# Two alpha loads move behind other transfers of SyncE's queue, their logarithms move later, and chunk 2's second row is prepared ahead of its first

## The chip, the core and the metric

The kernel runs on one NeuronCore of a Trainium2 chip. The core has five instruction streams that run side by side and meet only at semaphores: TensorE (PE, matrix products; its weight loads are listed apart as PEld), VectorE (DVE), ScalarE (ACT), GpSimd (POOL) and SyncE (SP), which here only issues transfers. Transfers are carried by 16 DMA engines. POOL's transfers stand in the profile as queue q0, SP's as q1. SBUF is the on-chip memory with 128 partitions; PSUM is the accumulator memory, here one tile of 8 banks of 512 float32 per partition.

The metric is the device time of one execution in microseconds (us). Lower is better.

## The reference

Two layers follow each other. The first is a gated linear attention, a recurrence over 768 time steps for 4 batches times 8 heads with a head dimension of 48:

```python
for t in range(S):
    state = alpha[:, :, t, :, None] * state + np.einsum('bhd,bhe->bhde', k[:, :, t], v[:, :, t])
    y[:, :, t] = np.einsum('bhd,bhde->bhe', q[:, :, t], state)
```

The second takes y as 3072 tokens of width 384 through a bilinear feed-forward layer of width 1536:

```python
a = x @ w_a
b = x @ w_b
return (a * b @ w_out)
```

q, k, v and alpha are 4 x 8 x 768 x 48 float32 (alpha between 0.8 and 1.0), w_a and w_b are 384 x 1536, w_out is 1536 x 384, and the output is 3072 x 384 float32.

## The kernel before

**Tiling.** The work is cut into six chunks, numbered 0 to 5. A chunk holds 256 time steps of two batches; the two batches are its "rows" 0 and 1 (the argument `u`, and `*` for both). Chunks 0 and 1 hold the first 256 steps of batches 0, 1 and of 2, 3; chunks 2 and 3 the next 256 steps; chunks 4 and 5 the last. A chunk thus needs the state that the chunk two before it left.

**One chunk, stage by stage.** The recurrence is turned into matrix products. The alphas of a chunk are loaded (`ld a`, line 413, one transfer of 768 KB for both rows) and their logarithms taken on ACT (`ln`, line 420). Pairs of neighbouring steps are added on DVE (`lx`, lines 433 and 436: three additions), split into a part that is exact in bf16 and two rests (`R 0` and `R 1`, line 497, on DVE: `lh` and `ll`), and summed along time by TensorE (`AQ`, line 507). Exponentials of the sums on ACT give the factors `beta` and `invb` (`E`, line 541). Queries and keys of even steps are first levelled with one alpha (`lv`, line 526, on POOL or DVE; `ra`, line 519, is the reciprocal that the queries take) and then multiplied by `beta` and `invb` on DVE (`mq` and `mk`, line 552), which gives the bf16 tile `QKp`. One transposing transfer per row, issued by SP (`T`, line 604), turns `QKp` into `kqT`. TensorE multiplies turned keys with turned queries (`D`, line 674); ACT or DVE take the result out of PSUM (`Mc`, line 683; `M`, line 679) and DVE applies the causal mask (`Mm`, line 687). TensorE also updates the state (`KA` or `K`, line 627; `k`, lines 662 and 663, on DVE) and forms y from the carried state (`SA`, `SB`, line 703) and from the masked scores (`Y`, line 724). ACT or DVE copy y out of PSUM as bf16 (`X`, lines 764 and 766), and a second kind of transposing transfer on SP (`XT`, line 771) turns it into `xT`, the input of the feed-forward layer.

The feed-forward layer of a chunk is 12 pieces of the hidden width. For each, `a` and `b` (line 786) fill one PSUM bank each, ACT copies the first (`as`, line 792), DVE multiplies it with the second (`pr`, line 800), and `o` (line 808) makes the output, which ACT or DVE copy (`ot`, lines 823 and 825) and SP stores (`st`, line 841).

**Order.** Nothing is scheduled by a planner. The order is written out by hand in the string `PROGRAM` at the top of the file: each line starts with a chunk number, then lists operations with their row, bank or engine (V is DVE, S is ACT, P is POOL, Y is SP). The program is recorded in that order, so every engine has its instructions in the order in which `PROGRAM` names them, and each engine works strictly in its order: an instruction that waits holds everything behind it on that engine. The framework adds the waits that the data and the buffers need. The feed-forward work of one chunk is mixed with the recurrence of the next, so that TensorE always has something to do.

**Names that the change touches.** The chunk's alpha tile `a_t` has two buffers: chunk 4's alphas take the place of chunk 2's, chunk 5's that of chunk 3's. The logarithms `la`, the pair sums, `lh` and `ll` have one buffer each. `gate_t` and `gate_m` (lines 858 to 864) are one-element copies on POOL into a scratch tile; they do no work, but POOL cannot pass them before the tile that they read is written:

```python
def gate_t(x, u):

    nc.gpsimd.tensor_copy(go, x.kqT[int(u)][0:1, 0, 0, 0, 0:1])
```

In `PROGRAM` the places that matter are lines 93 to 112 (end of chunk 2's preparation, beside chunk 1's feed-forward work), 135 to 163 (chunk 2's y, chunk 3's preparation, first part of chunk 2's feed-forward work), 166 to 182 (chunk 3's recurrence) and 194 to 206 (chunk 4's preparation ends, chunk 5's begins).

Of the kernel before, what the change touches and what calls it, by code (L numbers as in the profile page):

```python
# [92 lines left out]
1: a 7 0 3; b 11 0 1; pr 11 0; KA 1 64; k 1 0 V; k 1 1 V; b 10 0 5; a 10 0 7; as 10 0; a 0 0 6  # L93
2: lv 0 k V
1: pr 10 0; b 0 0 1; a 3 0 4; as 0 0; pr 0 0
2: lv 1 k P; mk 1 V
1: as 3 0; b 3 0 7; a 1 0 6; as 1 0
4: ld a * P
1: b 7 0 0; b 1 0 4; pr 1 0; as 7 0; pr 7 0; pr 3 0
2: mk 0 V  # L100
1: SB 1 0
3: ln *
1: a 6 0 2; as 6 0; b 9 0 3; a 4 0 5; a 9 0 6; as 9 0; pr 9 0
2: mq 1 V; T 1
0: o 2 0 4
1: b 4 0 6; b 6 0 7
2: lv 0 q P; mq 0 V
1: pr 6 0
2: T 0
3: ld k * Y  # L110
# [24 lines left out]
2: D 0 0 5; Mc 0 0; Mm 0 0 V; gatem 0 0; SB 0 1; SA 1; Y 1; X 1 S; XT 1  # L135
3: lv 0 k P; lv 1 k P
1: a 4 1 7
4: ln *
1: as 4 1; b 9 1 0; pr 9 1; o 0 0 5
3: AQ 3  # L140
2: SA 0; Y 0; X 0 S; XT 0
5: ld a * Y
1: o 0 1 -; ot 0 V; a 1 1 6; a 10 1 1; as 1 1; as 10 1
3: E 0 b; E 0 i
1: b 4 1 2; pr 4 1; b 8 1 5; b 1 1 1; a 8 1 6; b 10 1 0; pr 1 1; o 3 0 2; pr 10 1; as 8 1; pr 8 1; o 3 1 -; ot 3 S; st 3 Y
# [3 lines left out]
3: E 1 i  # L149
1: st 0 Y  # L150
3: dr
4: lx V; R 0
3: mk 0 V; mq 0 V; T 0
4: ld q * Y
2: a 1 * 2; b 5 * 0; as 5 *; pr 5 *
4: ra 1
2: b 7 * 4; b 10 * 1; pr 4 *; a 10 * 6; as 10 *; pr 10 *
3: mk 1 V
2: a 7 * 0; b 1 * 5; a 0 * 6; b 0 * 7; as 1 *; as 7 *; pr 1 *; pr 7 *; as 0 *; a 3 * 0; b 9 * 1; pr 0 *
3: mq 1 V  # L160
# [5 lines left out]
3: KA * 06; D 0 0 4; M 0 0; dl; k * 0 V; k * 1 V  # L166
1: o 1 0 2
2: b 11 * 7
5: ln *
2: a 11 * 5; as 11 *; pr 11 *  # L170
1: o 1 1 -; ot 1 S
2: a 6 * 5; as 6 *; a 8 * 3; as 8 *
3: SB 0 6; D 0 1 0; M 0 1; T 1
4: ld k * Y
3: D 1 0 4; Mc 1 0
2: b 6 * 2; pr 6 *; b 8 * 3; pr 8 *
4: R 1
# [16 lines left out]
3: a 11 * 5  # L194
2: ot 2 V; ot 3 V
4: mq 0 V; mk 0 V
5: lx V
3: a 9 * 3; a 0 * 2; a 8 * 6; b 11 * 7; as 9 *; as 11 *; as 0 *; pr 11 *; b 9 * 2; b 0 * 1; pr 9 *
5: lv 0 k V
3: as 8 *  # L200
# [70 lines left out]
def kernel(  # L271
# [11 lines left out]
    nc = tc.nc  # L283
# [17 lines left out]
    ld = ctx.enter_context(tc.tile_pool(name="ld", bufs=2))  # L301
# [21 lines left out]
    go = cst.tile([1, 1], F32, name="go")  # L323
    S0 = [cst.tile([C, B, D + P2 * VS], BF16, name=f"S0{i}") for i in range(2)]
    Sm = [cst.tile([C, 2, D + P2 * VS], BF16, name=f"Sm{i}") for i in range(2)]
    QKp = [cst.tile([C, 2, 2, 2, H, DP], BF16, name=f"QKp{i}") for i in range(2)]
# [9 lines left out]
    def const_fill():  # L336
        nc.vector.memset(wz, 0.0)
        nc.vector.memset(og, 0.0)  # L338
        for g in range(2):
            nc.vector.memset(og[g * HC:(g + 1) * HC, g:g + 1], 1.0)  # L340
# [517 lines left out]
    def gate_m(x, u, h):  # L858

        nc.gpsimd.tensor_copy(go, x.m[int(u), int(h)][0:1, 0, 0, 0, 0:1])  # L860

    def gate_t(x, u):

        nc.gpsimd.tensor_copy(go, x.kqT[int(u)][0:1, 0, 0, 0, 0:1])

    OPS = {
        "gatet": gate_t,
        "gatem": gate_m,
        "c1": lambda x: const_fill(),
        "c1a": lambda x: const_table(),  # L870
# [99 lines left out]
```

## Time and profile before

| What | Value |
|---|---|
| Median of 3 runs | 194.94 us (194.47 to 197.66) |
| The profiled execution, own time | 193.93 us |
| Its span, first to last instruction | 192.2 us |
| Granted TensorE clock, mean | 0.999 of full speed |
| Busy: PE / DVE / ACT / POOL | 184.1 / 136.1 / 103.1 / 50.1 us |
| Weight loads (PEld) | 111.3 us, beside PE |
| Moved by DMA | 30.96 MB, mean 161 GB/s |

The span leaves out what lies around the first and last instruction: 193.93 - 192.2 = 1.7 us. The busy times overlap, since the engines run side by side; the share that counts is that of the engine on which the end depends. In a row of the timeline the columns are: start in us from the span's start, length in us, engine, line of the kernel and operation, what it writes and reads, shapes, and how many instructions of a kind are merged into the row; in brackets stands how long the engine had been idle before and what released it. "SPq" is SP's own queue: the length of such a row is the time that SP spent on issuing, not the transfer's. A row of the list of transfers gives tile and source, issuing queue, count, size of each, and the median us from issue to landing.

### The profile page before, as it was taken

The numbers are of one execution on the slowest core, as the hardware profiler recorded it, in microseconds if no ns is written. First come the engines' busy times: TensorE is split into PE (matmuls) and PEld (weight loads), VectorE is DVE, ScalarE is ACT, GpSimd is POOL, SyncE is SP. The second block draws the span as 40 slices with busy tenths as digits, with TensorE's granted clock in tenths as the row PEclk, the third lists the DMA queues.
The fourth block names the chain that finished last, engine by engine and source line by source line (L and its number), as shares of the span: only waits on it lengthen the run. The fifth ranks groups of instructions, "written<-read, shape, count | busy, mean of one in ns | idle before, by whom it ended". The sixth has DMA issues, their size and how long they took to land.

```text
span 192.2 us, 5878 instructions
## 1 busy us (share of the span) xinstructions
PE 184.1 (96%) x2509; PEld 111.3 (58%) x2509; DVE 136.1 (71%) x230; ACT 103.1 (54%) x189; POOL 50.1 (26%) x72
## 2 busy tenths in 40 slices
PE   7979799999999998999999999999999999999993
PEld 3567576766777875644556644555544565544562
DVE  4778767999899796688979499864953961156520
ACT  4385566887585567446566135875266521164301
POOL 8999746920641404000400020050000000000000
PEclk9999999999999999999999999999999999999999
DMA  6999999999999999949993586998196005031013
GB/s 149 246 216 215 243 241 254 249 245 261 252 233 219 191 213 248 215 126 229 151 220 54 141 185 154 160 173 111 47 198 144 3 3 123 3 108 56 2 41 123
DMA packets 67162, 30.96 MB, mean 161 GB/s; under 512 B 58064, under 2 KB 65120, under 8 KB 67136
## 3 DMA queue, kind: packets, MB, share of 16 engines
q0 software_dynamic: 18640, 14.16, 41.9%
q1 hardware_dynamic: 48352, 16.34, 40.6%
q8 instruction: 19, 0.31, 0.7%
q10 hardware_dynamic: 144, 0.10, 0.2%
q14 instruction: 7, 0.06, 0.1%
HBM read 25.98 MB, written 4.74 MB: 160 GB/s over the span
## 4 chain that ended last, share of the span: by engine, by line
PE 86%; POOL 6%; DMA 4%; issue 1%; DVE 0%; ACT 0%; POOLq 0%; DVEq 0%
PE psum L786 48%; PE psum L808 24%; DMA wb_t<-in_moe_w_b_dram 4%; PE psum L674 3%; PE psum L724 2%; PE psum L627 2%; PE psum L698 2%; PE psum L703 1%; PE psum L507 1%; PE psum L819 1%; POOL v_t L413 1%; PE psum L593 1%; POOL a_t L413 1%; POOL wa_t L393 1%; POOL k_t L413 0%
## 5 line engine op out<-in xcount | busy, mean ns | idle before, releaser
L786 PE MATMUL psum<-xT,wb_t 128*128 128x512 bf16 (+1 forms) x270 | 57.0, 337 | 0.6 <-DMA wb_t<-in_moe_w_b_dram 0.5
L786 PE MATMUL psum<-xT,wa_t 128*128 128x512 bf16 (+1 forms) x270 | 56.1, 337 | 1.1 <-issue 0.7
L808 PE MATMUL psum<-wo_t,prod 128*128 128x384 bf16 x276 | 48.5, 326 | 0.0
L786 PEld LDWEIGHTS <-wb_t 128*128 128x128 bf16 x270 | 25.5, 98 | 21.1 <-DMA wb_t<-in_moe_w_b_dram 0.8
L786 PEld LDWEIGHTS <-wa_t 128*128 128x128 bf16 x270 | 25.6, 98 | 20.8 <-issue 1.0
L808 PEld LDWEIGHTS <-prod 128*128 128x128 bf16 x276 | 26.1, 98 | 16.9
L683 ACT ACTIVATE m<-psum 128x1024 bf16<-128x1024 f32 x16 | 16.3, 1023 | 6.5 <-PE psum L674 6.3
L825 DVE COPY ot<-psum 128x384 f32<-128x384 f32 (+1 forms) x13 | 6.9, 539 | 15.9 <-PE psum L808 13.4
L526 POOL TENSOR_TENSOR q_t<-q_t,ra 128x384 f32<-128x384 f32 x8 | 8.7, 1084 | 34.3 <-DMA q_t<-in_q_dram 17.3
L823 ACT ACTIVATE ot<-psum 128x384 f32<-128x384 f32 (+1 forms) x12 | 5.7, 477 | 12.9 <-PE psum L808 11.9
L420 ACT ACTIVATE la<-a_t 128x1536 f32<-128x1536 f32 (+2 forms) x9 | 9.5, 1057 | 3.4 <-DMA a_t<-in_alpha_dram 3.4
L687 DVE TENSOR_TENSOR m<-m,mask 128x1024 bf16<-128x1024 bf16 x16 | 10.8, 685 | 0.3 <-ACT m L683 0.3
L679 DVE TENSOR_TENSOR m<-psum,mask 128x1024 bf16<-128x1024 f32 x8 | 9.8, 1222 | 1.7 <-PE psum L674 1.5
L526 POOL TENSOR_TENSOR k_t<-k_t,a_t 128x384 f32<-128x384 f32 x5 | 5.3, 1064 | 19.0 <-DVE QKp L552 17.5
L552 DVE TENSOR_TENSOR QKp<-k_t,invb 128x768 bf16<-128x768 f32 x10 | 9.9, 992 | 0.2
L552 DVE TENSOR_TENSOR QKp<-q_t,beta 128x768 bf16<-128x768 f32 x10 | 9.3, 949 | 0.0
L674 PE MATMUL psum<-kqT 64*64 64x128 bf16 x384 | 8.6, 218 | 0.5 <-DVE prod L800 0.2
L413 POOL DMA_DIRECT2D v_t<-in_v_dram x8 | 8.6, 1070 | 0.5 <-issue 0.4
L674 PEld LDWEIGHTS <-kqT 64*64 64x64 bf16 x384 | 6.3, 107 | 3.2 <-issue 2.1
L764 ACT ACTIVATE ys<-psum 128x768 bf16<-128x768 f32 x7 | 5.6, 809 | 4.3 <-PE psum L703 2.3
L413 POOL DMA_DIRECT2D a_t<-in_alpha_dram x6 | 6.3, 1042 | 4.0 <-DMA wa_t<-in_moe_w_a_dram 2.2
L446 PE MATMUL psum<-wz 128*128 128x512 bf16 x17 | 5.5, 472 | 1.2 <-DVE og L338 1.2
(273 smaller groups left out, 270.9 us busy)
## 6 DMA issues: line engine op xcount, KB each, us to landing
out_dram<-ot SPq DMA_DIRECT2D x23, 192.0 KB, 2.2
a_t<-in_alpha_dram POOLq DMA_DIRECT2D x3, 768.0 KB, 14.5
k_t<-in_k_dram SPq DMA_DIRECT2D x3, 768.0 KB, 7.2
q_t<-in_q_dram POOLq DMA_DIRECT2D x2, 768.0 KB, 13.0
v_t<-in_v_dram POOLq DMA_DIRECT2D x4, 384.0 KB, 10.1
q_t<-in_q_dram SPq DMA_DIRECT2D x2, 768.0 KB, 6.6
a_t<-in_alpha_dram POOLq DMA_DIRECT2D x3, 384.0 KB, 5.6
q_t<-in_q_dram POOLq DMA_DIRECT2D x3, 384.0 KB, 13.4
```

Of the source, the lines that this page charges most:

```text
L413: eng.dma_start(out=t[:, us, hs].rearrange("p b h r d -> p (b h) (r d)"), in_=src[ch.b0 + us.start:ch.b0 + us.stop, hs, ch.s * 2 * C:(ch.s ...
L420: nc.scalar.activation(out=ch.la[:, us, hs].rearrange("p b h r d -> p (b h r d)"), in_=ch.a[:, us, hs].rearrange("p b h r d -> p (b h r d) ...
L526: eng.tensor_mul(x, x, by)
L552: eng.tensor_mul(QKp[ch.c % 2][:, u, j, :, hs, :D], src[:, u, hs].rearrange("p h r d -> p r h d"), f)
L674: nc.tensor.matmul(s2[g * HC:(g + 1) * HC, r, p, rk, :], lhsT=ch.kqT[u][rs, 1, rk, 2 * h + p, g * HC:(g + 1) * HC], rhs=queriesT(ch, u, 2 ...
L679: nc.vector.tensor_mul(m.rearrange("p r a k s -> p (r a) (k s)"), ch.s2[u, h].rearrange("p r a k s -> p (r a) (k s)"), maskn(4))
L683: nc.scalar.activation(out=m.rearrange("p r a k s -> p (r a) (k s)"), in_=ch.s2[u, h].rearrange("p r a k s -> p (r a) (k s)"), func=AF.Copy)
L687: eng.tensor_mul(x, x, maskn(4))
L786: nc.tensor.matmul(p, lhsT=(wa_t, wb_t)[w][:, kk, f * 128:(f + 1) * 128], rhs=ch.xT[:, us.start // 2:us.stop // 2, kk].rearrange("p u g s ...
L808: nc.tensor.matmul(op, lhsT=ch.prod[:, f, at:at + C], rhs=wo_t[:, f, :], start=(f == 0), stop=(f == NFF - 1))
L823: nc.scalar.activation(out=o_, in_=i_, func=AF.Copy)
L825: eng.tensor_copy(o_, i_)
```

## The change

Five things move; no arithmetic is added or removed.

- The load of chunk 4's alphas leaves POOL, where it stood behind the levelling of chunk 2's keys, and goes to SP behind the two transposing transfers of chunk 2's y. Chunk 5's alphas, which SP loaded there, go further back on SP, behind the load of chunk 4's keys and so ahead of the transposing transfers of chunk 3's y.
- The logarithms of chunk 4 (ACT) and their pair sums (DVE) move from ahead of chunk 3's multiplications into chunk 2's feed-forward work; the first rest (`R 0`, DVE) moves behind chunk 3's first scores. `R 1` and all that follows stay.
- The logarithms of chunk 5 move from chunk 3's state update to directly ahead of their pair sums, behind chunk 4's factors.
- In chunk 2, row 1's queries are multiplied and its `QKp` turned before row 0's keys are multiplied.
- A new gate on POOL waits for chunk 2's row 1 keys in `QKp` before POOL levels row 0's queries.

TensorE's instructions keep their order.

```diff
@@ PROGRAM, chunk 2's preparation @@
 1: a 7 0 3; b 11 0 1; pr 11 0; KA 1 64; k 1 0 V; k 1 1 V; b 10 0 5; a 10 0 7; as 10 0; a 0 0 6
 2: lv 0 k V
 1: pr 10 0; b 0 0 1; a 3 0 4; as 0 0; pr 0 0
-2: lv 1 k P; mk 1 V
+2: lv 1 k P; mk 1 V; gatek 1; lv 0 q P
 1: as 3 0; b 3 0 7; a 1 0 6; as 1 0
-4: ld a * P
 1: b 7 0 0; b 1 0 4; pr 1 0; as 7 0; pr 7 0; pr 3 0
-2: mk 0 V
+2: mq 1 V; T 1
 1: SB 1 0
 3: ln *
 1: a 6 0 2; as 6 0; b 9 0 3; a 4 0 5; a 9 0 6; as 9 0; pr 9 0
-2: mq 1 V; T 1
+2: mk 0 V
 0: o 2 0 4
 1: b 4 0 6; b 6 0 7
-2: lv 0 q P; mq 0 V
+2: mq 0 V
 1: pr 6 0
 2: T 0
 3: ld k * Y
@@ chunk 2's y, chunk 3's preparation @@
 3: lv 0 k P; lv 1 k P
 1: a 4 1 7
-4: ln *
 1: as 4 1; b 9 1 0; pr 9 1; o 0 0 5
 3: AQ 3
 2: SA 0; Y 0; X 0 S; XT 0
-5: ld a * Y
+4: ld a * Y
 1: o 0 1 -; ot 0 V; a 1 1 6; a 10 1 1; as 1 1; as 10 1
...
 3: dr
-4: lx V; R 0
 3: mk 0 V; mq 0 V; T 0
 4: ld q * Y
 2: a 1 * 2; b 5 * 0; as 5 *; pr 5 *
-4: ra 1
-2: b 7 * 4; b 10 * 1; pr 4 *; a 10 * 6; as 10 *; pr 10 *
+4: ln *; ra 1
+2: b 7 * 4; b 10 * 1; pr 4 *
+4: lx V
+2: a 10 * 6; as 10 *; pr 10 *
 3: mk 1 V
@@ chunk 3's recurrence @@
 2: b 11 * 7
-5: ln *
 2: a 11 * 5; as 11 *; pr 11 *
 1: o 1 1 -; ot 1 S
 2: a 6 * 5; as 6 *; a 8 * 3; as 8 *
+4: R 0
 3: SB 0 6; D 0 1 0; M 0 1; T 1
 4: ld k * Y
+5: ld a * Y
 3: D 1 0 4; Mc 1 0
@@ chunk 5's preparation @@
 4: mq 0 V; mk 0 V
-5: lx V
+5: ln *; lx V
@@ the new gate @@
+    def gate_k(x, u):
+
+        nc.gpsimd.tensor_copy(go, QKp[x.c % 2][0:1, int(u), 1, 0, 0, 0:1])
+
+        "gatek": gate_k,
```

## The prediction

> **What bounds the kernel now.** I read the page's head and the shares of the chain that ended last first, then that chain in order of time.
>
> ```profile
> span 192.2 us, 5878 instructions
> PE 184.1 (96%) x2509; PEld 111.3 (58%) x2509; DVE 136.1 (71%) x230; ACT 103.1 (54%) x189; POOL 50.1 (26%) x72
> ...
> PE 86%; POOL 6%; DMA 4%; issue 1%; DVE 0%; ACT 0%; POOLq 0%; DVEq 0%
> ```
>
> TensorE is the bound: busy 184.1 of 192.2 us. Nothing else holds over 1% of the chain except POOL and the DMA, whose parts, as the chain shows, lie before 22.6 us. So an edit to loads, logarithms or queues can only move the end through an idle gap of TensorE that it closes or opens. The chain shows where those gaps are (start, length, what):
>
> ```profile
> 22.61 0.05 issue
> ...
> 60.63 4.96 PE psum L786 x45
> ...
> 66.14 0.63 PE psum L674 x32
> ...
> 76.32 0.72 issue
> ...
> 98.65 0.46 PE psum L674 x32
> ...
> 104.42 0.51 PE psum L724 x32
> ...
> 110.88 9.06 PE psum L786 x42
> ```
>
> From 22.6 us on the chain is TensorE's own work, with two gaps: one from 60.63 + 4.96 = 65.59 to 66.14, and one of 0.72 at 76.32 in which TensorE waits for nothing that the profile shows. The first lies inside the region of the change. Together they are 1.3 us: that is about all that the change can win.
>
> **Row 1 first, and the load off POOL.** The gap at 65.6 is the first use of chunk 2's turned row 1. The timeline from 44 to 62 us shows what leads up to it:
>
> ```profile
> 54.54 0.95 DVE L552 TENSOR_TENSOR QKp<-k_t,invb 128x768 bf16<-128x768 f32 x1
> ...
> 54.70 1.19 POOL L413 DMA_DIRECT2D a_t<-in_alpha_dram  x1 [1.89 <-DVE prod L800]
> ...
> 55.92 1.02 POOL L526 TENSOR_TENSOR q_t<-q_t,ra 128x384 f32<-128x384 f32 x1
> ...
> 56.07 0.44 DVE L800 TENSOR_TENSOR prod<-as__1149,psum 128x256 bf16<-128x256 bf16 x1
> ...
> 56.41 1.36 DVE L552 TENSOR_TENSOR QKp<-k_t,invb 128x768 bf16<-128x768 f32 x1
> ...
> 59.03 4.96 SPq L604 DMA_TRANSPOSE kqT<-QKp  x1
> ```
>
> and the one from 62 to 90 what waits for it, and three rows for the part on chunk 4:
>
> ```profile
> 66.12 0.48 PEld L674 LDWEIGHTS <-kqT 64*64 64x64 bf16 x32 [0.50 <-DMA kqT<-QKp]
> ...
> 80.08 0.55 DVE L433 TENSOR_TENSOR l<-la 128x384 f32<-128x384 f32 x1
> 80.64 1.12 DVE L436 TENSOR_TENSOR l<-la 64x384 f32<-64x384 f32 x2
> ...
> 81.79 0.96 DVE L497 TENSOR_TENSOR lh<-l 128x768 f32<-128x768 f32 x1
> ```
>
> Chunk 2's row 1 keys are multiplied at 54.54, but row 0's keys follow (1.36 us, 0.41 longer than the same work at 54.54, beside POOL's levelling), so row 1 goes out to be turned only at 59.03. It is there at 66.12, 7.1 us later, and TensorE's weight load has lost 0.50. Beside it run POOL's transfers, the alphas of chunk 4 (issued 54.70) among them. In the changed order row 1's queries follow the three products that end at 56.07 + 0.44 = 56.5, and take 0.95 (1.36 if POOL runs beside them): issue at 57.5 to 57.9. Landing is bounded by this same row (7.1 us, the alphas in the way) and by the list of transfers:
>
> ```profile
> a_t<-in_alpha_dram POOLq DMA_DIRECT2D x3, 768.0 KB, 14.5
> k_t<-in_k_dram SPq DMA_DIRECT2D x3, 768.0 KB, 7.2
> ...
> a_t<-in_alpha_dram SPq DMA_DIRECT2D x1, 768.0 KB, 6.4
> ...
> kqT<-QKp SPq DMA_TRANSPOSE x8, 4.8
> xT<-ys SPq DMA_TRANSPOSE x8, 3.0
> ```
>
> With 4.8 it lands at 62.3, with 7.1 at 65.0, both before 65.6, when TensorE asks. So the 0.50 goes whole. What is late next: row 0's turn. Its keys and queries now follow row 1's, so it is ready at about 57.9 + 0.44 + 2 x 0.95 = 60.2, and SP, held 4.96 by row 1 at worst, issues it by 62.9, where before it was 59.03 + 4.96 = 64.0; nothing waited for it then, nothing will.
>
> The gate costs POOL the copy of one element and a wait until the keys are done at 55.5. Behind it stands row 0's levelling (1.02), done by 56.7, and its reader now comes at 59. The 1.19 of issue that POOL loses would be worth that much only if someone waited there; nobody does. Cost of both: nothing.
>
> **Chunk 4's logarithms and sums.** SP's own rows, and ACT's and DVE's from 82 us on:
>
> ```profile
> 77.30 0.45 SPq L413 DMA_DIRECT2D a_t<-in_alpha_dram  x1
> ...
> 91.42 2.33 SPq L604 DMA_TRANSPOSE kqT<-QKp  x1
> 93.86 0.53 SPq L413 DMA_DIRECT2D k_t<-in_k_dram  x1
> 102.83 4.33 SPq L771 DMA_TRANSPOSE xT<-ys  x2
> ```
>
> ```profile
> 83.17 0.62 ACT L792 ACTIVATE as__1812<-psum 128x512 bf16<-128x512 f32 x1
> ...
> 86.46 0.60 ACT L792 ACTIVATE as__1828<-psum 128x512 bf16<-128x512 f32 x1 [2.27 <-PE psum L786]
> ...
> 92.79 1.48 ACT L420 ACTIVATE la<-a_t 128x1536 f32<-128x1536 f32 x1
> ...
> 105.83 0.52 ACT L541 ACTIVATE beta<-psum 128x384 f32<-128x384 f32 x1
> 112.21 0.60 ACT L792 ACTIVATE as__2319<-psum 128x512 bf16<-128x512 f32 x1 [5.85 <-PE psum L786]
> ```
>
> ```profile
> 85.22 0.71 DVE L800 TENSOR_TENSOR prod<-as__1780,psum 128x512 bf16<-128x512 bf16 x1
> 87.09 0.73 DVE L800 TENSOR_TENSOR prod<-as__1828,psum 128x512 bf16<-128x512 bf16 x1 [1.16 <-ACT as__1828 L792]
> ...
> 92.27 0.73 DVE L800 TENSOR_TENSOR prod<-as__1870,psum 128x512 bf16<-128x512 bf16 x1 [0.28 <-ACT as__1870 L792]
> ...
> 98.94 1.22 DVE L679 TENSOR_TENSOR m<-psum,mask 128x1024 bf16<-128x1024 f32 x1 [1.02 <-PE psum L674]
> ...
> 103.23 0.68 DVE L687 TENSOR_TENSOR m<-m,mask 128x1024 bf16<-128x1024 bf16 x1
> ```
>
> Chunk 4's alphas take the place of chunk 5's on SP: issued at 77.30, in 83.7 (6.4). The logarithm (1.48) stands on ACT behind the row at 83.17, which ends at 83.8. So ACT does not wait, and the logarithm falls into the 2.27 us of idle time that end at 86.46 (from 84.19, reciprocal done): 2.27 - 1.48 leaves 0.8 of cover.
>
> On DVE 0.55 + 1.12 + 0.96 = 2.63 leave 80 to 82.7 us, where TensorE sets the pace: no gain. The sums (1.67) come back at 85.22 + 0.71 = 85.93, end at 87.60, and push the row at 87.09 by 0.51. The 0.28 of idle at 92.27 leaves 0.23 of it. The rest (0.96) comes back ahead of the row at 98.94, whose 1.02 of idle covers it but for 0.17 with the delay. The last mask for row 1, at 103.23, then ends at 103.91 + 0.17 = 104.08, and TensorE asks for it at 104.42: 0.34 to spare. This is the tightest place on DVE. Row 1 of chunk 3 goes to be turned up to 0.5 later than 91.42 and lands, at 4.8, by 96.8; it is used in the second half of TensorE's row at 98.65. All these times move with TensorE, so the spare stays when TensorE comes 0.5 earlier.
>
> **Chunk 5's alphas and logarithms.** SP issues the load at 94.4, behind the keys of 93.86; SP is free until 102.83, so the 0.45 costs nothing there. The logarithm leaves 92.79 and stands behind the row that ends at 106.35, where ACT is idle for 5.85: the alphas need only be in by 110.7. What it can delay is chunk 3's turned y, whose two issues take 1.2 us each of SP's time:
>
> ```profile
> L771 SPq DMA_TRANSPOSE xT<-ys x8: 1210/1219/1823, 73.1 to 159.9; - x8
> ```
>
> The second is issued at 102.83 + 4.33 - 1.21 = 105.95 and lands, by 3.0, at 109.0; TensorE asks at 110.88. Spare: 1.9.
>
> **The sum.** 0.50 won, all else covered: the span goes from 192.2 to 191.7, and the profiled execution from 193.93 to 193.4. That execution lies 1.0 below the median of the runs, 194.94; carried over to the median, the forecast is **194.4 us**.
>
> **Rivals.**
>
> *The alphas come late (slower).* The load of chunk 4 is issued at 77.30 instead of 54.70, 6.5 us before ACT wants it. The sums on DVE start at 85.93, so the alphas must be in by 85.93 - 1.48 = 84.45, and with the 0.34 to spare at 104.4 by 84.8: 7.5 us after issue. From there on each microsecond stops ACT, then DVE, then TensorE one for one. The row of its own slot says 6.4 and that of SP's keys 7.2, both inside; POOL's 14.5 would give 194.4 + 7.0 = 201.4. Against it: SP's queue has no long row of this size. Chance 0.13, most of it for one or two us (195.4 to 196.4), 0.04 for more.
>
> *Turned y behind the alphas (hardly a gain, or slower).* The keys issued at 93.86 land by 101.1 (7.2). If chunk 5's alphas, on the same SP queue, move only behind them, they land 6.4 later, at 107.5, and the two transposing transfers behind those at 107.5 + 3.0 + 1.2 = 111.7: 0.8 later than asked. Time 194.4 + 0.8 = 195.2. For it: both transfers and the turn are q1's. Against: the worst of three durations is taken each time. Chance 0.10.
> [...]
>
> *The gap stays (no change).* If the turn of row 1 is held by the queries of chunk 3, still POOL's, rather than by the alphas, and takes over 7.7 us, nothing is won: 194.9. Against: 7.1 was with both in the way. Chance 0.10.
>
> *The gap at 76.32 goes as well.* It has no cause in the profile; if it came from the full DMA queues, which the change thins out before it, 0.72 more: 193.7. Chance 0.08.
>
> **How the numbers follow.** The forecast keeps 0.59. What a measurement of this kernel can tell from no change is about 2%, 3.9 us: two gaps of 1.3 us cannot give that, so faster 0.01; slower needs alphas some 4 us late or two mishaps at once: 0.04; same 0.95. The range reaches from both gaps closed with the runs' lower scatter (193.7 less 0.5, from 194.94 to 194.47: 193.2) to alphas two us late (196.4).
>
> **What would show it.** Right: no idle time of TensorE before its first line 674 row near 65.6; that row's turn issued near 57.5; the logarithm of chunk 4 starting near 83.3 with no wait for `a_t`; line 724 near 103.9 and line 786 near 110.4 without a gap. Wrong: ACT waiting for `a_t` near 84 with TensorE idle behind it, a gap at 104 or 110, or the gap at 65.6 still there.

## The result: 1.1% slower, and a new gap at 105 us

| | before | after |
|---|---|---|
| Median of the runs taken side by side (6 each) | 195.13 us | 197.00 us |
| Ratio after to before, 95% interval | | 1.0112 (1.0083 to 1.0142) |
| The profiled execution, own time | 193.93 us | 196.72 us |
| Its span | 192.2 us | 194.9 us |

The change costs 1.6 to 2.8 us, where 0.5 less was forecast. One of the six runs of before, 197.66 us, was slow, over 1.5% above the fastest of its kernel, and the ratios here and below leave such runs out.

The head of the page of after and its instruction queue (packets, MB, share of the 16 DMA engines' time that the packets took):

```profile
span 194.9 us, 5882 instructions
PE 185.7 (95%) x2509; PEld 112.7 (58%) x2509; DVE 135.4 (69%) x230; ACT 103.5 (53%) x189; POOL 48.6 (25%) x72
...
q8 instruction: 19, 0.31, 0.7%
```

TensorE is still the bound. The chain that ended last, of after (start, length, what):

```profile
61.77 5.28 PE psum L786 x48
67.05 0.57 PE psum L674 x32
...
100.80 0.24 PE psum L703 x16
101.05 0.23 PE psum L674 x16
101.28 0.12 PE psum L703 x16
101.39 0.51 PE psum L724 x32
101.90 2.06 PE psum L808 x12
103.96 0.63 PE psum L507 x8
104.59 0.12 PE psum L703 x14
104.71 0.38 PE psum L724 x21
105.09 2.36 issue
107.44 0.30 PE psum L724 x11
107.75 5.96 PE psum L808 x36
```

Both gaps of before are gone: 61.77 + 5.28 = 67.05, so TensorE goes from the feed-forward products straight into the turned row 1, and no row of 0.7 us stands near 76. In their place stands one of 2.36 us at 105.09, in the middle of the 32 products of line 724: 21 of them, the pause, then 11. The waits of TensorE (us in total, times, longest), first of after, then of before:

```profile
PE psum L724 <- issue: 2.4, 1, 2.4
```

```profile
PE psum L786 <- issue: 0.7, 1, 0.7
...
PE psum L674 <- DVE prod L800: 0.2, 1, 0.2
```

So the new gap is of the same kind as the 0.72 that the prediction left unexplained: "issue", a wait for nothing that the profile shows. The second row of before prices the other gap, at 65.6, at 0.2 where the prediction read 0.50, and puts it down to a product of DVE, not to the turned row 1. The covers that the prediction counted on did hold, as the timeline of after shows (ACT, DVE and SP, with the idle time before the row in brackets):

```profile
84.54 1.49 ACT L420 ACTIVATE la<-a_t 128x1536 f32<-128x1536 f32 x1 [0.46 <-DMA a_t<-in_alpha_dram]
...
107.70 1.48 ACT L420 ACTIVATE la<-a_t 128x1536 f32<-128x1536 f32 x1 [1.05 <-DMA a_t<-in_alpha_dram]
...
103.53 0.69 DVE L687 TENSOR_TENSOR m<-m,mask 128x1024 bf16<-128x1024 bf16 x1
...
95.24 4.76 SPq L413 DMA_DIRECT2D a_t<-in_alpha_dram  x1
103.13 6.99 SPq L771 DMA_TRANSPOSE xT<-ys  x2
```

Both logarithms waited for their alphas, by 0.46 and 1.05 us, and both waits vanished in ACT's idle time: no gap of TensorE follows them. The last mask ends at 104.22, and TensorE began its line 724 at 104.71.

**What moves at that moment.** The program loads more at 101 to 106 us than before. The DMA queues in one microsecond each (packets, MB, share), of after from 103 to 104 and from 104 to 105:

```profile
q1 hardware_dynamic: 789, 0.30, 120.3%
...
q1 hardware_dynamic: 656, 0.25, 121.6%
q8 instruction: 1, 0.02, 7.5%
```

and of before from 101 to 102:

```profile
q0 software_dynamic: 71, 0.01, 15.6%
q8 instruction: 1, 0.02, 6.4%
```

q8 is the queue that the page names instruction. The 19 packets of the page are 0.31 MB, so 16 KB each, and 19 for 2509 products with as many weight loads makes some 264 instructions for each. In before the packet came at 101 to 102, when little else moved. In after it came at 104 to 105, beside chunk 5's alphas, which SP had issued at 95.24 behind chunk 4's keys and whose last packet starts at 107.05. Counted from the trace, the gap of before at 76 lies behind TensorE's product 1245 and that of after behind product 1629. 1629 - 1245 = 384 = 3 x 128: both are at a border of blocks of 128 products with their 128 weight loads, 256 instructions.

**Theory**, the author's assumption from these counts and times, which the runs below test: TensorE's instructions arrive in blocks of 256. The next block is fetched only when TensorE crosses into the current one; in before it crosses at 100.56 and the packet starts at 101.14, in after at 100.85 and 104.57. A block of products lasts 4.05 us here if they are as short as those from 100.85 to 104.91. If the DMA engines are full (q1's packets 121.6% from 104 to 105 in after), the packet starts late, TensorE runs out of instructions, and pauses at the border, in after until 107.44, 2.87 us behind the packet's start. **Rivals:** a semaphore or an operand at these products; SP's queue being held up; an accident of one execution; or a loss at the start, since the feed-forward layer's products, the mixture below, get under way 1.1 us later in its profile (TensorE's product 299, counted from 0, at 23.79 instead of 22.65 us).

### The profile page after: what moved, and what is told of

Its sections match the earlier page's. It is cut to its first block, busy times and chain, and to the rows that moved or that the text cites. A ratio compares the mean times of both kernels' runs of the same rounds, so it can differ in the third digit from the quotient of the medians.

```text
span 194.9 us, 5882 instructions
## 1 busy us (share of the span) xinstructions
PE 185.7 (95%) x2509; PEld 112.7 (58%) x2509; DVE 135.4 (69%) x230; ACT 103.5 (53%) x189; POOL 48.6 (25%) x72
## 4 chain that ended last, share of the span: by engine, by line
PE 85%; POOL 6%; DMA 5%; issue 2%; ACT 0%; POOLq 0%
PE psum L786 48%; PE psum L808 24%; DMA wb_t<-in_moe_w_b_dram 5%; PE psum L674 3%; PE psum L724 2%; PE psum L627 2%; PE psum L698 2%; PE psum L703 1%; PE psum L507 1%; PE psum L819 1%; POOL v_t L413 1%; PE psum L593 1%; POOL a_t L413 1%; POOL wa_t L393 1%; POOL k_t L413 0%
## 5 line engine op out<-in xcount | busy, mean ns | idle before, releaser
L724 PE MATMUL psum<-v_t,m 64*128 64x48 bf16 x256 | 4.6, 180 | 2.4 <-issue 2.4
```

The source lines that it names most:

```text
L724: nc.tensor.matmul(y[:, g, h * D:(h + 1) * D], lhsT=ch.m[u, h // 4][gs, h % 2, h // 2 % 2, rk, :], rhs=value(ch, gs, u, rk, h), start=not ...
```

## The experiments

In the times below "the gap" is the distance between the starts of two neighbouring products in the trace; 0.0 to 0.1 is no gap at these borders.

### Moving the borders

Products of 64 columns that nobody reads replaced four fillers at the start of after, so that TensorE has 100 products more, which by the theory moves every border against the work. 128 more would move it by a whole block, back to the same product.

```diff
-fill 9 2;
+fill 5 2; tiny 104 2;      (100 more products; 132 in the control, 128 more)
```

> The changed kernel with 100 more pairs of weight load and matrix product on TensorE at the very start (four of the 512-column fillers are replaced by 104 products of 64 columns that nobody reads), nothing else. The gap of 2.5 us stands between TensorE's pairs 1629 and 1630 counted from 0; the gap of 1.0 us of the kernel before stands between its pairs 1245 and 1246, which is 3 x 128 pairs earlier, and three of the 16 KB instruction transfers lie between. Theory 'fetch': TensorE's instructions come in blocks of 128 pairs, and a block that is asked for when the DMA engines are full comes too late. Moving the borders by 100 pairs puts them where TensorE needs over 5.6 us for each block from 93 us on, so the gap at 105 goes (under 0.3 us left) and the time falls by about 2 us, to 194.5 to 195.5, unless the tiny products delay the start (up to 1 us). A smaller gap may come up near 71, where one block still lasts only 4.6 us. Rival 'data': TensorE waits for something that belongs to that product (masks, values) and that the profile does not name. Then the gap stays at the same product of line 724, about 2.4 us, and the time stays at 197.

> The control of the run with 100 pairs: 128 pairs more, so the borders of the blocks of 128 pairs come to lie at the same instructions as in the changed kernel. Theory 'fetch': the gap stays inside the second product group of line 724 in chunk 3, 1.5 to 3 us at about 105, and the time at about 197. Rival 'data': the same here; but if it is merely the added products that move things, this run shows it, since they are nearly the same as with 100 pairs.

With 100 more the pause at line 724 near 105 is gone (distance 0.00 where it was 2.54; the borders, now elsewhere, show at most 0.33 from 60 to 110 us), and the time is 195.70 us, ratio 1.0023 (0.9987 to 1.0059), 0.2 above what was expected. The mixture starts late, at 24.17 us, and a border that now falls behind product 477 has a pause of its own, of 0.65:

```profile
27.06 0.47 issue
```

With 128 more the pause at line 724 stays, behind product 1629 + 128. The median of that run is 200.28 us and in its profile the mixture starts at 26.84, some 3 us late, so its time decides nothing and only the place is read; from there to the last product it takes 168.17 us, after 167.34 to 168.13. Its chain:

```profile
108.68 0.38 PE psum L728 x21
109.06 1.85 issue
110.90 0.30 PE psum L728 x11
```

Line 728 is line 724 here, and it breaks after the same 21 products. Neither an operand nor a semaphore can tell 100 from 128. The same in the kernel before, moved by 100 later and by 16 earlier:

```diff
-fill 9 2;
+fill 5 2; tiny 104 2;
```

> The kernel before with the same 100 extra pairs at the start as in the earlier run of the changed kernel. Theory 'fetch': the 1.0 us gap behind TensorE's pair 1245 near 76 is one of the same kind, so it goes (under 0.4 left at the shifted border), while the 0.5 at 65.6, a wait for the turned row 1, stays. In the changed kernel the extra pairs made the start some 1.7 us later, so the time is 195.0 to 196.5 here. Rival 'data': the gap stays at the same product.

```diff
-0: ... fill 7 2; ... fill 9 2; ... fill 1 1; ...
+0: ... fill 1 2; ...
```

> The kernel before with 16 of the 17 filler products of its start (512 columns each, they feed nothing) left out; nothing else of the computation. Every later product has an index lower by 16, so the borders of the 128-pair blocks of TensorE's instructions fall 16 products later in the kernel. Theory (instructions fetched behind loads): the 0.72 to 0.99 us behind product 1245 disappear from that place, and no gap over 0.4 us appears at the new border 16 products later unless the DMA traffic there is as heavy; if nothing goes at the start, about 194.0 (ratio 0.995). Rival (the gap belongs to this point of the work: a semaphore, a queue, the product's operands): the gap of 0.7 stays where it is, in front of the same product, 194.9 (ratio 1.000). The fillers may also have hidden something at the start; then the first products of chunk 0 begin later and the ratio rises above 1 with both theories, and the place of the gap alone decides.

The gap at the old place went both times (0.11 for 0.99). With 100 more two new ones came at borders, 0.94 behind product 477 and 1.46 in line 728, `L728 <- issue` in its waits:

```profile
25.93 0.75 issue
...
72.81 1.28 issue
```

With 16 fewer the borders from 73 to 81 us show 0.44 and 0.11, and TensorE loses 0.61 in waiting for DVE at 65 us and 0.66 for chunk 2's turned y at 82.5. Neither is a gain in time: 196.48 (ratio 1.0095, 1.0059 to 1.0131) and 196.16 (1.0054, 1.0024 to 1.0083). Without the fillers the mixture (product 299 of before) starts at 24.56 us, where three profiles of before have 22.65 to 23.10, so 194.0 for that run was wrong.

### Changing the traffic

One part alone (chunk 5's alphas and logarithms moved, all else as before), the other (row 1 first with its gate, loads as before), and after without that load:

```diff
-5: ld a *  Y              (behind chunk 2's turned y)
+5: ld a *  Y              (behind chunk 4's keys; ln 5 later, as in the change)
```

> The kernel before with one part of the change alone: chunk 5's alphas are loaded behind chunk 4's keys and their logarithms taken ahead of the pair sums. Chunk 4's alphas stay on GpSimd, row 0 stays first, no gate. Theory 'fetch': the instruction block that TensorE asks for near 100.5 us meets this load, so a gap of 1.5 to 2.7 us opens at 105 behind TensorE's pair 1629, while the old gaps of 0.5 at 65.6 and about 1 at 76 stay: 196.4 to 197.6, ratio 1.008 to 1.014. Rival 'the rest of the change costs it' (the later logarithms and sums of chunk 4, the order of the rows): no new gap, 194.5 to 195.3.

```diff
+2: mq 1 V; T 1            (ahead of mk 0; gatek 1; lv 0 q P behind "4: ld a * P")
```

> The kernel before with the other part alone: in chunk 2 row 1's queries are multiplied and turned first, with the gate on GpSimd; the loads and logarithms of chunks 4 and 5 stay where they were. The step of the prediction on row 1: its turn is issued near 57.5 instead of 59.0 and lands before 65.6, so the 0.5 us gap there goes; the gap at 76 may stay. Time 194.0 to 194.8, ratio 0.995 to 0.999. If the load of chunk 4's alphas had to leave for this, the turn takes over 8 us and the gap stays: ratio 1.000.

```diff
-5: ld a * Y
+5: rea                    (chunk 5 takes chunk 3's alphas)
```

> The changed kernel without the load of chunk 5's alphas: chunk 5 works on chunk 3's alphas, which are still in their buffer; so 0.79 MB are not moved. Theory 'fetch': with nothing but keys and values on the DMA engines between 95 and 105, the instruction block asked for at 101 is there in time, no gap at 105, time 194.0 to 195.0. If the loss came from the order of the logarithms and sums on ScalarE and VectorE instead, which is unchanged here, the gap or the loss stays: 196.5 to 197.5.

Chunk 5's load alone gives 196.73, ratio 1.0096 (1.0059 to 1.0134), nearly the whole loss. Its chain has both gaps, the old and the new:

```profile
76.74 0.76 issue
...
105.25 1.48 issue
```

Left out, it gives 193.90, ratio 0.9959 (0.9927 to 0.9992), and the gap shrinks from 2.54 to 1.07; it does not vanish as expected, since 0.67 MB still moved in the 4 us, 0.45 of them chunk 4's keys. Row 1 first alone gives 195.19, ratio 0.9999 (0.9972 to 1.0027). Its chain:

```profile
58.76 8.73 DMA kqT<-QKp
67.54 0.64 PE psum L675 x32
...
77.76 0.68 issue
```

The turn is issued at 58.76, 1.1 us earlier than in before if counted from product 299, but takes 8.73 us beside POOL's loads, and lands later than TensorE asks (distance 1.06). Preparing row 1 first bought nothing with chunk 4's alphas left on POOL.

The same load in two other places, directly behind chunk 4's, and on POOL instead of SP:

```diff
+4: ld a * Y; 5: ld a * Y   (at 79 us)
```

> The changed kernel, with the load of chunk 5's alphas directly behind that of chunk 4's on SyncE (near 78 us) instead of behind chunk 4's keys (near 95 us). All else as changed. Theory 'fetch': no load of that size runs near 101 us when the block is asked for, so the gap at 105 goes and the time is 194.0 to 195.2. The turn of chunk 3's row 0 (issued near 84.5) is then behind 1.5 MB on SyncE's queue and lands near 91 instead of 89, used at 93.5: a small risk. Rival 'data' with the masks or values as the cause: the gap stays, 197.

```diff
+5: ld a * P                (behind "4: ld v * P")
```

> The changed kernel with chunk 5's alphas loaded by GpSimd behind chunk 4's values (issued near 95) instead of by SyncE behind chunk 4's keys (near 95): the same bytes at the same time on the other queue. Theory 'fetch, by the amount of traffic': the block asked for near 101 is late as well, gap 1 to 2.7 us, 195.5 to 197.2. Rival 'fetch, by the SyncE queue alone' (the turned y of chunk 3 pile up behind the load on the same queue): the gap shrinks to that without the load, about 1 us or less, and the turned y land earlier: 194 to 195.3.

Behind chunk 4's alphas: 195.52, ratio 1.0037 (1.0012 to 1.0062), and the gap is 1.23 where none was expected, while chunk 4's keys were pushed back to 97.16 in turn; behind product 1434 the distance is 1.19 instead of 0.31, where a small transfer of chunk 3 (`bl`) comes late (5.33 us on the chain, at most 4.2 to land in before). On POOL: 197.21, ratio 1.0104 (1.0065 to 1.0142), with the largest gap of all:

```profile
105.14 2.62 issue
```

There SP's queue holds no load of chunk 5's alphas, so its order is not the cause; the amount under way, 1.04 MB in the 4 us behind the crossing, is that of after (0.98 to 1.06).

### Taking the load out of the way without leaving it out

```diff
-5: ld a * Y                (95 us)
-5: ld k * Y
+5: ld a * Y; ld k * Y      (107 us; ln, lx, R 0 and lv 0 k of chunk 5 later)
```

> The kernel after, with the load of chunk 5's alphas moved on SP from behind chunk 4's keys (95 us) to directly ahead of chunk 5's keys (about 107 us, behind chunk 3's turned y), and chunk 5's logarithms, sums, R 0 and level values after that. Nothing is left out. Theory (instructions fetched behind loads): at 101 us, where TensorE crosses into the block ahead of the border at line 724, only the tail of chunk 4's keys is under way, so the gap at 105 falls from 2.4 to 1 us or less, as when that load is left out (0.9); the next block is crossed into at about 105 and lasts 15 us, which covers any delay: 193.8 to 194.8 (ratio 0.994 to 0.999), if the late sums do not stop TensorE near 125. Rival (SP's order or chunk 4's keys make the gap): 2.4 us stay, 197 (ratio 1.010). If the late logarithms do stop TensorE, a wait for a_t, la or l shows near 120 to 130 us and the time rises by its length, and the gap at 105 still decides between the two.

The gap at 105 closes (0.38), but 198.02, ratio 1.0155 (1.0107 to 1.0203). The second rival of that text came true as well; the timeline of ACT and DVE:

```profile
117.03 1.49 ACT L418 ACTIVATE la<-a_t 128x1536 f32<-128x1536 f32 x1
...
118.56 0.56 DVE L431 TENSOR_TENSOR l<-la 128x384 f32<-128x384 f32 x1 [2.32 <-ACT la L418]
```

The late sums stand ahead of chunk 3's products on DVE, and TensorE pauses 0.82 us near 118 and 2.77 near 120. Putting the logarithms and sums still further back:

```diff
-5: ln *; lx V; R 0         (near 117)
-5: lv 0 k V
+5: ln *                    (ahead of chunk 4's K)
+5: lx V; lv 0 k V          (behind chunk 3's as 10)
+5: R 0                     (ahead of chunk 3's pr 10)
```

> As the run before it (chunk 5's alphas loaded directly ahead of chunk 5's keys), with chunk 5's logarithms moved further back, to directly ahead of chunk 4's turns near 120 us, its sums, level values and R 0 behind chunk 3's products near 130 us, where the kernel after has idle time on ACT and DVE. Nothing is left out. Theory (instructions fetched behind loads; the 2.8 us near 120 were only DVE's order): no gap over 0.5 us at 65.6, 76, 105 or 120, so the three gaps of before (0.5, 0.7 to 1.0) stay closed without a new one: 193.4 to 194.4 (ratio 0.992 to 0.998). Rival (late alphas of chunk 5 cannot be covered): a wait of TensorE on la, lh or QKp of chunk 5 between 120 and 150 us, time 195 or more. Rival (SP's order): the gap of 2.4 us at line 724 near 105 is back, 197.

195.45, ratio 1.0016 (0.9994 to 1.0039). No gap over 0.5 at 65.6, 76, 105 or 120. The chain at 105:

```profile
104.64 0.38 PE psum L723 x21
105.02 0.16 issue
105.17 0.31 PE psum L723 x11
```

The whole change is in this kernel, and only the load of chunk 5 and its logarithms stand elsewhere. What was won at the borders it loses at 131.5, where the distance is 1.10 and TensorE waits for DVE's mask. Taking DVE's work from that stretch:

```diff
-5: lx V; lv 0 k V
+5: lx V; lv 0 k P
-5: R 0                     (130 us)
+5: R 0; R 1                (133 us)
```

> As the run before it, but chunk 5's level-0 keys are worked by POOL instead of DVE and its R 0 goes directly ahead of R 1, behind chunk 4's last mask: 1.5 us of DVE's work leave the stretch from 126 to 132 us, in which TensorE waited 1.1 us for chunk 4's masks and sums. Nothing is left out. Theory (DVE's order made that wait, the instruction blocks are no longer in the way): no gap over 0.5 us from 60 us on, 193.8 to 194.6 (ratio 0.994 to 0.999). Rival (something else holds it there, or the gap at 105 is the load's and comes back): 195.4 or more (ratio 1.001 or more).

196.75, ratio 1.0081 (1.0053 to 1.0110): wrong. The gap at 105 stays small (0.61), but DVE is slower where POOL now works beside it (timeline):

```profile
126.74 1.82 DVE L434 TENSOR_TENSOR l<-la 64x384 f32<-64x384 f32 x2
...
129.23 1.70 DVE L685 TENSOR_TENSOR m<-m,mask 128x1024 bf16<-128x1024 bf16 x1
...
128.27 1.15 POOL L524 TENSOR_TENSOR k_t<-k_t,a_t 128x384 f32<-128x384 f32 x1
129.39 0.98 POOL L524 TENSOR_TENSOR q_t<-q_t,ra 128x384 f32<-128x384 f32 x1
```

In the run before it the same two took 1.12 and 0.68, with 0.50 of the mask beside POOL there too. This is one profile, whose own time of 198.02 lies above that kernel's median, and POOL's rows overlap the sums by only 0.3 us, so that POOL makes the whole loss is not shown. The run before it shows the effect on its own, on the rest `lh` beside POOL and on `ll`, of the same shape, without it:

```profile
129.57 1.76 DVE L496 TENSOR_TENSOR lh<-l 128x768 f32<-128x768 f32 x1
...
132.46 0.95 DVE L496 TENSOR_TENSOR ll<-lh 128x768 f32<-128x768 f32 x1
...
129.16 1.35 POOL L525 TENSOR_TENSOR q_t<-q_t,ra 128x384 f32<-128x384 f32 x1 [1.20 <-DVE prod L799]
```

So no version here that loads everything beats the kernel before.

### Both kernels again

Each kernel was profiled twice more, unchanged:

> The kernel before, unchanged: how much of what one profile shows recurs. Theory (instructions fetched behind loads): a gap of 0.5 to 1.5 us behind product 1245 again, none behind product 1629, since the traffic at these places follows the program; the start (the first product of the mixture behind the weights, product 299) may differ by a microsecond, since it did among kernels that share the code there. Rival (the gaps are accidents of one execution): other places or none.

> The kernel after, unchanged. Theory: a gap of 1.5 to 3 us behind product 1629 again and less than 0.4 us behind product 1245, none for the turned row 1; from product 299 to the end 1.2 to 2.2 us more than in the kernel before, as in the first two profiles (167.8 against 166.1). Rival (the gap at 105 is an accident, the loss is at the start): no gap there, and a start 1 us later than the kernel before has.

> As the first repetition of the kernel before: the gap behind product 1245 again, none behind 1629; product 299 between 22.5 and 24 us.

> As the first repetition of the kernel after: the gap behind product 1629 again, of 1.5 to 3 us; product 299 between 22.5 and 24 us, no later on the mean than in the kernel before.

Own times 194.91 and 194.67 of before, 195.92 and 196.22 of after. The chains of after's second and third profile:

```profile
104.81 1.83 issue
```

```profile
105.12 1.81 issue
```

The three distances that differ by over 0.1 us on the mean, and the border at 1117, in us:

| behind product | before, three profiles | after, three profiles | mean difference |
|---|---|---|---|
| 936, the turned row 1 (0.20 is no gap) | 0.49, 0.20, 0.37 | 0.20, 0.20, 0.20 | -0.15 |
| 1117, a border | 0.02, 1.01, 0.02 | 0.32, 0.41, 0.49 | +0.06 |
| 1245, a border | 0.99, 0.81, 0.70 | 0.11, 0.11, 0.11 | -0.72 |
| 1629, a border | 0.00, 0.00, 0.00 | 2.54, 2.01, 1.99 | +2.18 |

The sum is +1.37. From product 299 to the last, before takes 166.08, 166.61 and 166.43 us and after 167.76, 167.34 and 168.13: a difference of the means of 1.37, so the four places are all of it. (The second profile of after is 0.97 above the mean of before, less than the 1.2 to 2.2 that was expected.) Product 299 itself starts at 22.65, 23.10 and 23.01 in before and at 23.79, 23.42 and 22.91 in after. That is 0.45 later on the mean, against the last expectation, but the starts scatter by 0.5 in before and by 0.9 in after. So a loss at the start is not shown, and it cannot be the 1.37. What stays open are some tenths: the interval of the runs is 1.6 to 2.8, and the borders carry 1.4.

**The fetch, border by border.** For the block crossed into near 101 (it lasts 4.05 us) the trace gives the traffic in the 4 us behind the crossing, when the instruction packet started after it, and the gap:

| kernel | MB in 4 us | packet starts after | gap |
|---|---|---|---|
| before, three profiles | 0.17 to 0.19 | 0.58 to 0.65 us | 0.00 |
| chunk 5's load late (three kernels) | 0.56 to 0.60 | 1.87 to 2.07 us | 0.34 to 0.61 |
| behind chunk 4's; left out | 0.64; 0.67 | 3.06; 2.63 us | 1.23; 1.07 |
| chunk 5's load alone moved | 0.91 | 3.01 us | 1.66 |
| after, three profiles | 0.98 to 1.06 | 3.52 to 3.72 us | 1.99 to 2.54 |
| on POOL | 1.04 | 3.98 us | 2.80 |

The border behind 1245 (4.84 us) has it the other way round: 1.00 to 1.08 MB, a packet after 3.22 to 3.63 and a gap of 0.70 to 0.99 in before; 0.57 to 0.60 MB, 1.60 to 1.83 and 0.11 in after.

The amount orders the kernels well at these two borders, but it is not the whole law. At the border behind 1117 (4.45 us) after has 1.18 to 1.24 MB, yet the packet starts after 2.44 to 2.64 us and the gaps are 0.32 to 0.49; in before 0.86 to 0.90 MB go with 1.61, 2.96 and 1.69 us and gaps of 0.02, 1.01 and 0.02. What sets the packet's start beyond the amount is open. What holds throughout is the step from packet to product: in the 18 profiles 31 gaps of over 0.3 us stand at borders behind 20 us, and at each of them TensorE goes on 2.2 to 2.9 us after the packet's start. A pause thus came where the packet's delay and these 2.2 to 2.9 us together exceeded the length of the block: in after 3.72 + 2.87 - 4.05 = 2.54. At each border in the table the packet starts behind the crossing. Elsewhere it can start ahead: in before by 0.7 and 2.0 us near 135 and 170 us. So "only when TensorE crosses" is shown for the borders of the table, not for all.

The table also shows 0.56 to 0.67 MB without chunk 5's load, where before has 0.17 to 0.19. In before the last packet of chunk 4's keys starts 0.1 to 0.3 us ahead of the crossing near 101; in the four kernels with that load left out or late it starts 2.3 to 3.8 us behind it. With row 1 first alone it is again 0.6 ahead. What is left to delay the keys into the fetch, and to add a smaller share to the gap, is the part on chunk 4's load and logarithms; this is argued, since no run has that part alone.

## Why the prediction was wrong

**The step that failed** is "The sum", with its "all else covered", and behind it the part on chunk 5's alphas. It asked only who waits for the load's data, for ACT's logarithm and for SP's queue, and found "SP is free until 102.83, so the 0.45 costs nothing there". What stood in the load's way was no data at all: TensorE's own instructions, which the page counts on the same 16 DMA engines (q8, 0.7% of their time), fetched at a time when before was nearly quiet (0.17 to 0.19 MB in 4 us, against 0.98 to 1.06 in after). Cost: 2.18 on the mean, and 1.66 with that load and its logarithms moved alone. The rival on the turned y had the traffic right: it let the alphas land at 107.5, and the last packet of their load starts at 107.05. It asked of that traffic only what it does to other data.

**Row 1 first, 0.50.** The gap went, but the term was mis-sized: 0.29 in that profile and 0.15 on the mean of three. The chain there left TensorE for DVE after 45 of the 48 products of line 786 (after's chain shows all 48 in 5.28), so the last three were counted as idle; the row of 0.50 was idle time of the weight load, whose last one ahead of it started 0.1 before its product (65.53 and 65.63), and the waits of PE said 0.2. The cause is open. Before has the 0.20 that is no gap in one of its three profiles, and so have three other kernels with the old order and chunk 4's alphas on POOL: chunk 5's load alone moved, 100 products more, 16 fewer. The new order alone did not help (8.73 us for the turn, 1.06 for the distance); the load off POOL has no run with the old order.

**Chunk 4's logarithms and sums.** Right in what it asked: the wait for the alphas (0.46) and the sums stayed under cover, and no gap came at 104.4 for the masks. *The alphas come late* did not happen: they were in by 84.54, inside the prediction's limit of 84.8. What it did not ask is where the delay of chunk 3's row 1 (turned at 92.17 instead of 91.42) puts the load of chunk 4's keys, which SP issues behind it.

**Turned y behind the alphas.** Not seen as a stop of TensorE, which came 2.36 late itself. The second transposing transfer of line 771 went out at 108.8 instead of 105.95 and the two held SP 6.99 instead of 4.33. By the prediction's 3.0 to land, that is 111.8; TensorE would have asked at 113.71 - 2.36 = 111.35. That the rival would have cost 0.5 without the gap is argued, not shown.

**The gap at 76.32 goes as well.** Given 0.08, and it was right, with its reason, "if it came from the full DMA queues, which the change thins out before it": 0.72 won on the mean. The prediction used that reason only where the change empties the queues and did not ask where it fills them. The unexplained row was the key to both signs.

The prediction's end named "a gap at 104 or 110" as a sign that it is wrong. One came, at 105, but the prediction had late masks in mind there, and they were on time. A change within 2% was right; the time, 2.6 us above the forecast, lies outside the range, which ended at 196.4.

## What to carry to other kernels

A row "issue" on the bounding engine that waits for nothing visible should be explained before anything is moved: count the instructions between two such rows (here 768 from the one of before to that of after, three packets of 16 KB), and if they are whole blocks apart, look for the instruction queue's packet and at what the DMA engines carry beside it. When a load is moved, ask not only who needs its data and whose queue it holds, but also whether the bounding engine runs through many short instructions while it is under way (here 256 in 4.05 us); a place 12 us later, over a stretch of long products (a block of 15.8 us), cost the next border nothing (0.01). And read a small gap in several profiles, and from the waits of the engine itself, before it is counted as a gain.

## What the runs showed of the hardware

- TensorE paused at borders of 256 instructions: 128 short products with their weight loads were used up in 4.05 us, and the next block's packet started 0.6 us after the crossing with 0.17 to 0.19 MB moving in 4 us (before, no pause), but 3.5 to 4.0 us with about 1.0 MB (after, and the load on POOL: pauses of 1.99 to 2.80). At 31 gaps in 18 profiles TensorE went on 2.2 to 2.9 us after the packet's start. The amount alone did not fix the start: at another border of after 1.18 to 1.24 MB went with 2.44 to 2.64 us.
- A transposing transfer of one row of `QKp`, 4.8 us at the median of before, took 8.73 us beside POOL's loads with row 1 first alone, and 7.1 in the same place of before.
- With POOL at work beside it, DVE's `lh` took 1.76 us, and 0.95 us was enough for `ll`, of the same shape, without it (one profile); a mask took 1.70 beside two operations of POOL in one run and 0.68 in the run before, of which 0.50 lay beside POOL too. So work moved from DVE to POOL was not free for DVE in these profiles, but what it cost is not shown.
- The same start-up code puts product 299 anywhere from 22.65 to 23.79 us in six profiles of two kernels, more than the gain that was forecast.
